# Spatial-weight sums by column blocks, attention without a forced end, and a z2 product among the last bands

## The chip, the cores and the metric

One core of one Trainium2 chip. The metric is device time of one execution, in microseconds (us); several executions of each kernel are timed in turn with the kernel before. Engines: PE is the tensor engine, DVE the vector engine, ACT the scalar engine, SP the engine whose queue issues nearly all loads and stores.

## The reference

Two blocks share 2048 tokens of width 1024, and a sigmoid gate mixes them:

```
g = sigmoid((x * gate_w).sum(-1))
A: qkv = x @ wqkv; 32 heads; each token attends to 8 earlier tokens, 2 apart; softmax; o @ wo
B: z = gelu(x @ w_in); z1 = z[..., :1792]; z2 = layernorm(z[..., 1792:])
   b = (z1 * (w_sp @ z2 + b_sp)) @ w_out
out = g * a + (1 - g) * b
```

w_sp is 2048 x 2048, the "spatial weights". Inputs and outputs are bfloat16.

## The kernel before

The large products run as Strassen-like quads: seven half-size products whose operands are sums and differences, made on DVE. Each product of a quad ends in a PSUM bank that ACT or DVE must read before PE may use that bank again (in the trace of the kernel before, PE waits 0.3 us each for L421, L474 and L487). In the profiles L403 is a matmul of such a product; L421, L427 and L487 are ACT's and L474 is DVE's work on its bank. A band set is a batch of attention's score products (L355), which ACT copies (L363), and which are stored to HBM (band_d) and loaded again. L1178 (L1192 in the changed kernel) is the gelu of z1. The stages overlap: attention of head group g (eight groups, four heads each) is computed on DVE and ACT while PE already projects the next group, then z2, then z1. Instruction order is fixed when the program is built: a list scheduler with a clock for each engine places DVE work between PE products.

z1 has seven steps, numbered here from the first to the seventh (fp = 0 to 6 in the code). Beside these, the spatial weights are loaded by eight transposing transfers and combined on DVE.

```python
def products():                      # attention: weights times v, then the tree of sums
    ...
    for ws in SPLIT[g > FINE]:       # FINE is -1: slices of 2, 2048 elements
        ... tt(p5[:, ws], in0[:, ws], in1[:, ws], ALU.mult)                # the "L677" of the profile
    for n, ws in enumerate([slice(0, 4)] if g <= FINE else [slice(0, 2), slice(2, 4)]):
        ... tt(a, a, b, ALU.add)                                           # L681
    ...                                                                    # L682, L686

BAND_AT = (1, 3, 6)                  # after which products of a quad a band set stands
...
return [tiles[0], band[1], tiles[1], band[0], tiles[2], band[2], tiles[3]] # group 7

def load_raw(c, a):                  # one of eight transposing loads of w_sp
    row = 4 * c + (a % 4) + 8 * (a // 4)
    inst = sync.dma_start_transpose(raw_slots[c][:, :, a, :], wsp_v[row])
...
z1s_slots = [... for o in (T1_OFF, R_OFF + 16384)]     # z1_quad uses z1s_slots[fp == 3]
...
RAW_AT = {2: {2: 0, 4: 1}, 3: {2: 2, 4: 3, 6: 4}, 4: {2: 5, 4: 6, 6: 7}}
for fp in range(NFH):
    ...
    if fp == SUMS:                   # the sixth step
        fill.extend((clock["PE"] + RAW_IN, 1.15, f) for f in wsp_sums(0, 0))
    ...
    run(z1_quad(fp, 0), z1_quad(fp, 1), hooks=hooks, step=lambda: z1_step(fp, at))
    if fp == DRAIN:                  # after the second step: all that is left of attention
        drain()
    ...                              # loads of w1, stores of z1
    if fp == NFH - 3:
        load_rows()                  # b_sp and og, after the fifth step
```

The gelus of all z1 steps but the fourth write one buffer, from which the step's result is stored to HBM (z_d); the next step's gelus must wait until that store has landed (5.6 us in two waits in the kernel before). And the weights land in the buffers that attention used, so no transpose may start before attention's last result (o_d) is stored (SP waits 4.8 us for it in the kernel before).

## Time and profile before

| | before |
|---|---|
| time, median of 3 runs (of 6, with the changed kernel) | 650.38 us (650.45) |
| span of the profiled run | 649.2 us |
| PE busy | 638.1 us, 98% |
| DVE / ACT busy | 519.3 / 297.8 us |
| listed PE waits between 50 and 640 us | 0.6 + 0.3 + 0.3 + 0.3 + 0.3 us |

PE is the bound nearly everywhere, so a change is judged by where PE stands on the clock, and by the waits that bind it.

The table "position" below is made so: the start of the same ACT copy out of PSUM (they follow PE's products) in one trace, less its start in the trace of the kernel before.

### The profile page before, as it was taken

To read this page: it belongs to the slowest core of one execution; us is meant where nothing else is said; L and a number is where in the kernel's file an instruction comes from. 1 tells how busy PE (TensorE), PEld (TensorE's weight loads), DVE (VectorE), ACT (ScalarE), POOL (GpSimd) and SP (SyncE) were. 2 spreads that over 40 slices of the span, in tenths; PEclk is the share of its full clock that TensorE was granted. 3 is DMA by queue.
4 is the path that set the end of the run, shared out by engine and by line. 5 is a ranking of instruction groups with operands and counts; after the bars stand their busy time and mean duration, and the time that the engine had idled before them with its cause. 6 is when DMAs were issued, how large, how long until landed. Compare 5 with 4: busy or idle time off the path is not lost.

```text
span 649.2 us, 11298 instructions
## 1 busy us (share of the span) xinstructions
PE 638.1 (98%) x4346; PEld 336.4 (52%) x4391; DVE 519.3 (80%) x816; ACT 297.8 (46%) x644; POOL 15.4 (2%) x27
## 2 busy tenths in 40 slices
PE   8999999999999999999999999999999999999997
PEld 4544467444445555444444444444444444868684
DVE  0357988999899999999988766987569999596952
ACT  3547677676776877799643121121121121212110
POOL 2210000000000000001000000000000000000000
PEclk9999999999999999999999999999999999999999
DMA  9979564798688012258994578469587383665401
GB/s 207 198 179 269 126 152 103 175 230 200 122 214 204 1 42 85 66 148 230 258 269 133 130 163 172 120 195 280 100 189 172 86 157 99 111 138 128 124 27 49
DMA packets 227174, 98.19 MB, mean 151 GB/s; under 512 B 174496, under 2 KB 214064, under 8 KB 227120
## 3 DMA queue, kind: packets, MB, share of 16 engines
q1 hardware_dynamic: 226256, 95.70, 61.2%
q0 software_dynamic: 576, 1.57, 0.9%
q8 instruction: 34, 0.56, 0.3%
q10 hardware_dynamic: 288, 0.20, 0.1%
q14 instruction: 20, 0.16, 0.1%
HBM read 44.31 MB, written 36.61 MB: 125 GB/s over the span
## 4 chain that ended last, share of the span: by engine, by line
PE 84%; ACT 4%; DVE 4%; DMA 4%; SPq 2%; issue 2%; ACTq 0%; DVEq 0%
PE psum_all L403 69%; PE psum_all L1487 8%; PE psum_all L293 4%; PE psum_all L303 2%; DMA band_d<-arena 2%; ACT arena L839 2%; PE psum_all L355 1%; DVE arena L677 1%; ACT arena L1178 1%; SPq L189 1%; DVE arena L681 1%; SPq L178 1%; DMA arena<-in_A_wqkv_dram 1%; SPq L194 1%; DVE psum_all L474 1%
## 5 line engine op out<-in xcount | busy, mean ns | idle before, releaser
L403 PE MATMUL psum_all<-arena 128*128 128x512 f16 (+6 forms) x2482 | 503.0, 362 | 3.4 <-issue 0.6
L403 PEld LDWEIGHTS <-arena 128*128 128x128 f16 (+1 forms) x2518 | 245.1, 98 | 253.8 <-issue 4.0
L677 DVE TENSOR_TENSOR arena<-arena,att_A 128x2048 f16<-128x2048 bf16 x64 | 75.5, 1219 | 0.3
L474 DVE TENSOR_TENSOR psum_all<-psum_all,arena 128x512 f32<-128x512 f32 (+1 forms) x78 | 51.0, 669 | 10.1 <-PE psum_all L403 8.3
L1487 PE MATMUL psum_all<-arena 128*128 128x256 f16 (+1 forms) x468 | 51.6, 273 | 0.0
L1487 PEld LDWEIGHTS <-arena 128*128 128x128 f16 x468 | 45.8, 98 | 5.5
L293 PE MATMUL psum_all<-arena 128*128 128x512 bf16 x183 | 42.0, 379 | 1.4 <-issue 0.8
L421 ACT COPY psum_all<-psum_all 128x512 f32<-128x512 f32 (+1 forms) x24 | 12.5, 521 | 66.8 <-PE psum_all L403 66.2
L784 ACT ACTIVATE arena<-psum_all 128x448 bf16<-128x448 f32 x64 | 34.3, 546 | 19.0 <-PE psum_all L403 9.0
L1178 ACT ACTIVATE arena<-psum_all 128x512 bf16<-128x512 f32 x56 | 31.4, 612 | 19.8 <-PE psum_all L403 9.0
L681 DVE TENSOR_TENSOR arena<-arena 128x2048 f16<-128x2048 f16 x32 | 37.9, 1218 | 0.0
L363 ACT CAST arena<-psum_all 128x1988 f16<-128x1988 f32 (+3 forms) x25 | 34.0, 1360 | 3.6 <-PE psum_all L355 3.4
L839 ACT ACTIVATE arena<-arena 128x896 bf16<-128x896 bf16 x32 | 30.9, 980 | 0.0
L546 DVE TENSOR_TENSOR arena<-arena 128x512 f16<-128x512 bf16 (+5 forms) x60 | 30.1, 534 | 0.3
L445 ACT COPY psum_all<-psum_all 128x512 f32<-128x512 f32 (+1 forms) x24 | 12.4, 519 | 37.2 <-PE psum_all L403 36.6
L293 PEld LDWEIGHTS <-arena 128*128 128x128 bf16 x192 | 18.1, 98 | 21.6 <-DMA arena<-in_A_wqkv_dram 0.7
L870 ACT CAST arena<-psum_all 128x512 bf16<-128x512 f32 x40 | 22.1, 592 | 12.5 <-DVE psum_all L474 9.6
L389 DVE TENSOR_TENSOR arena<-arena 128x2048 f16<-128x2048 bf16 x8 | 9.4, 1222 | 21.8 <-ACT gl_s L306 20.9
L427 ACT COPY arena<-psum_all 128x512 f32<-128x512 f32 (+1 forms) x24 | 12.7, 534 | 26.3 <-PE psum_all L403 22.5
L487 ACT COPY psum_all<-psum_all 128x512 f32<-128x512 f32 (+1 forms) x39 | 21.7, 570 | 6.6 <-PE psum_all L403 6.0
L432 ACT COPY psum_all<-psum_all 128x512 f32<-128x512 f32 (+1 forms) x24 | 12.5, 519 | 25.6 <-PE psum_all L403 23.0
L550 DVE TENSOR_TENSOR arena<-arena 128x1024 f16<-128x1024 f16 (+1 forms) x16 | 11.3, 714 | 15.7 <-PE psum_all L403 15.7
(113 smaller groups left out, 530.6 us busy)
## 6 DMA issues: line engine op xcount, KB each, us to landing
arena<-v_d SPq DMA_DIRECT2D x8, 960.0 KB, 7.1
z_d<-arena SPq DMA_DIRECT2D x14, 512.0 KB, 3.4
arena<-z_d SPq DMA_DIRECT2D x14, 512.0 KB, 4.1
zg_d<-arena SPq DMA_DIRECT2D x56, 128.0 KB, 2.2
arena<-zg_d SPq DMA_DIRECT2D x32, 224.0 KB, 3.2
band_d<-arena SPq DMA_DIRECT2D x28, 248.5 KB, 4.6
arena<-in_A_wqkv_dram SPq DMA_DIRECT2D x16, 256.0 KB, 4.3
o_d<-arena SPq DMA_DIRECT2D x4, 1024.0 KB, 6.3
```

Source lines behind the costliest of these rows:

```text
L293: nc.tensor.matmul(ps[:], w[:, t, kt, :], xT[:, kt, 512 * c:512 * (c + 1)], start=(kt == 0), stop=(kt == KT - 1))
L363: nc.scalar.copy(dst, src)
L403: nc.tensor.matmul(bank[:, 0:N], lhsT, rhs, start=(start and m == 0), stop=(m == n - 1), skip_group_check=True)
L474: last_add[0] = nc.vector.tensor_tensor(out[:, n], a[:, n], vs, ALU.add)
L546: return [lambda a=a: nc.vector.tensor_tensor(*a) for a in args]
L677: lambda ws=ws, in0=in0, in1=in1: tt(p5[:, ws], in0[:, ws], in1[:, ws], ALU.mult)), False
L681: lambda a=p3[:, ws], b=p3[:, ws.start + 4:ws.stop + 4]: tt(a, a, b, ALU.add)), not n
L784: nc.scalar.activation(z2[:, i + 8 * a, ZC * c:ZC * (c + 1)], bank[:, 0:ZC], ACT.Gelu_apprx_tanh, accum_out=s1[:, 4 * n + c:4 * n + c + 1])
L839: return nc.scalar.activation(junk, src, ACT.Square, accum_out=(s2, s2h)[x][:, n:n + 1])
L870: nc.scalar.copy((qT_slots, kT_slots)[t][g % 2][:, :, 256 * (c + 2 * x):256 * (c + 2 * x + 1)], bank[:].rearrange("p (n e) -> p e n", e=2))
L1178: last_gelu[0] = nc.scalar.activation(z1s[:, f, a, :], bank[:], ACT.Gelu_apprx_tanh)
L1487: nc.tensor.matmul(bank[:, h], l, r, start=(start and m == 0), stop=(m == len(ab) - 1), skip_group_check=True)
```

## The change

Its intent: to take out the small PE waits in groups 2 and 7, to let attention's DVE work run out among the z1 steps in place of a forced end that stops everything else, and to begin the sums of the spatial weights by column block, each as soon as its two loads have landed.

```diff
-                for ws in SPLIT[g > FINE]:
+                for ws in SPLIT[not wide[0]]:                 # wide in groups 5, 6, 7: 4096 elements
...
-            if n + 1 in BAND_AT:
+            if n + 1 in (BAND_AT if g != 2 else (1, 3, 5)):
...
-        return [tiles[0], band[1], tiles[1], band[0], tiles[2], band[2], tiles[3]]
+        early.append(z2_quad(*quads[0], 0))
+        return [tiles[0], band[1], tiles[1], lambda: next(early[0]), band[0], tiles[2], band[2], tiles[3]]
...
+        two = [z2_quad(*q, m) for m, q in enumerate(quads[n:n + 2])]
+        if n == 0:
+            two = [two[1], early[0]]
...
         if c == 0:
-            for n in (0, 4):        # halves
...
+            lo, hi = slice(P * part, P * part + P), slice(512 + P * part, 512 + P * part + P)
+            a, b, e, t1 = raw[:, 0:8, lo], raw[:, 0:8, hi], raw[:, 8:16, hi], t_sum[0][:, :, lo]
+            yield lambda: tt(t1, b, a, ALU.subtract)
+            yield lambda: tt(half[:, 0:8, hi], e, b, ALU.subtract)
...
     def z1_step(fp, at):
         step()
         at[0] += 1
+        since[0] += 1
+        if raws and since[0] >= 3 and not due and all(s[1] == () for s in streams):
+            load_raw(0, raws.pop(0))
+            since[0] = 0
+            if len(raws) % 2 == 0:
+                pair = 3 - len(raws) // 2
+                raw_in[0] = max(raw_in[0] + 4.5, clock["PE"] + 8.0, z3[0] + 8.0)
+                fill.extend((raw_in[0], 0.61, f) for f in wsp_sums(0, pair))
+                fill.sort(key=lambda x: x[0])
...
-    RAW_AT = {2: {2: 0, 4: 1}, 3: {2: 2, 4: 3, 6: 4}, 4: {2: 5, 4: 6, 6: 7}}
...
-        if fp == DRAIN:
-            drain()
```

`streams` are attention's three queues of DVE work: the first transpose is placed once they are empty, the next ones at least three products apart.

More of the change, by code (lines that the diff above doesn't have):

```diff
@@ L678, in products @@
                 multiplied.add((g, e))
-                for n, ws in enumerate([slice(0, 4)] if g <= FINE else [slice(0, 2), slice(2, 4)]):
+                for n, ws in enumerate([slice(0, 4)] if wide[0] else [slice(0, 2), slice(2, 4)]):
                     yield now, 0.068 + 0.533 * (ws.stop - ws.start), (
@@ L692, in products @@
             next_v()
+    wide = [False]
     SPLIT, FINE = [[slice(n * x, n * x + n) for x in range(8 // n)] for n in (4, 2)], FINE_TO
@@ L785, in z2_gelu, with z2_tile @@
                              accum_out=s1[:, 4 * n + c:4 * n + c + 1])
-    def z2_tile(i, a, m):
-        ps = low_bank()
+    def z2_tile(i, a, m, bank=low_bank):
+        ps = bank()
         pe(2 * T_Z)
@@ L912, in play_group @@
         return True
+    early = []
     def group_tiles(g):
@@ L917, in group_tiles @@
         else:
-            tiles = [lambda a=a, m=m: z2_tile(7, a, m) for m in range(2) for a in range(2)]
+            roles = bank_roles[0]
+            tiles = [lambda n=n: z2_tile(7, n % 2, n // 2, lambda: roles[3 - n % 2]) for n in range(4)]
         if g == 0:
@@ L1030 @@
         hold[0] = g == NG - 1
+        wide[0] = g in (5, 6, 7)
         paired = play_group(g)
@@ L1050 @@
             play(main[8 - (not g):])
+    wide[0] = False
     load_later(1, clock["PE"] + 3.0, 2.0)
@@ L1065, in quad_step @@
         def quad_step():
-            hold[0] = count[0] != 1
-            if n == 0 and count[0] == 0:
-                mark(bank_roles[1][1:3], ZC)
+            hold[0] = count[0] != 4
             step()
@@ L1073, in quad_step @@
                 square(*squares.pop(0), None)
-        run(*[z2_quad(*q) for q in quads[n:n + 2]], step=quad_step)
+        two = [z2_quad(*q, m) for m, q in enumerate(quads[n:n + 2])]
+        if n == 0:
+            two = [two[1], early[0]]
+            next(early[0])
+            quad_step()
+            mark(bank_roles[1][1:3], ZC)
+        run(*two, step=quad_step)
     hold[0] = False
@@ L1130, in wsp_sums @@
         if c == 0:
-            for n in (0, 4):
-                i, hi = slice(n, n + 4), slice(8 + n, 12 + n)
-                a, b, d, e = raw[:, i, 0:512], raw[:, i, 512:1024], raw[:, hi, 0:512], raw[:, hi, 512:1024]
-                t1, t2, t3 = (t[:, i] for t in t_sum)
-                if part == 0:
-                    yield lambda t1=t1, a=a, b=b: tt(t1, b, a, ALU.subtract)
-                    yield lambda b=b, e=e, h=half[:, i, 512:1024]: tt(h, e, b, ALU.subtract)
-                else:
+            if part == 4:
+                for n in (0, 4):
+                    i, hi = slice(n, n + 4), slice(8 + n, 12 + n)
+                    d, e = raw[:, hi, 0:512], raw[:, hi, 512:1024]
+                    t1, t2, t3 = (t[:, i] for t in t_sum)
                     yield lambda t1=t1, t2=t2, e=e: tt(t2, e, t1, ALU.subtract)
                     yield lambda t2=t2, t3=t3, d=d: tt(t3, d, t2, ALU.subtract)
+                return
+            lo, hi = slice(P * part, P * part + P), slice(512 + P * part, 512 + P * part + P)
+            a, b, e, t1 = raw[:, 0:8, lo], raw[:, 0:8, hi], raw[:, 8:16, hi], t_sum[0][:, :, lo]
+            yield lambda: tt(t1, b, a, ALU.subtract)
+            yield lambda: tt(half[:, 0:8, hi], e, b, ALU.subtract)
         elif part == 0:
@@ L1193 @@
     ready = [0]
+    raws, since, raw_in = [0, 4, 1, 5, 2, 6, 3, 7], [0], [0.0]
+    z3 = [0.0]
     def z1_step(fp, at):
@@ L1197, in z1_step @@
         at[0] += 1
+        since[0] += 1
[6 more added lines that the diff above has]
+                fill.extend((raw_in[0], 0.61, f) for f in wsp_sums(0, pair))
+                fill.sort(key=lambda x: x[0])
         if at[0] % 2 == 0 and squares:
@@ L1205, in z1_step @@
         if fp == NFH - 1 and at[0] == 2:
-            fill.extend((0.0, 1.15, f) for f in wsp_sums(0, 1))
+            fill.extend((0.0, 1.15, f) for f in wsp_sums(0, 4))
     mark([b[1] for b in bank_roles], 512, ZC)
@@ L1210 @@
     RAW_IN = 3.0
-    DRAIN, SUMS = 1, NFH - 2
-    RAW_AT = {2: {2: 0, 4: 1}, 3: {2: 2, 4: 3, 6: 4}, 4: {2: 5, 4: 6, 6: 7}}
+    SUMS = NFH - 2
     for fp in range(NFH):
@@ L1218 @@
         if fp == SUMS:
-            fill.extend((clock["PE"] + RAW_IN, 1.15, f) for f in wsp_sums(0, 0))
+            assert not raws
+        z3[0] = clock['PE'] + 12.0 * (3 - fp) + 12.0
         late = () if fp else [b[2] for b in bank_roles]
         at = [0]
-        hooks = {3: lambda: mark(late, 512, ZC), **{n: lambda a=a: load_raw(0, a) for n, a in RAW_AT.get(fp, {}).items()}}
+        hooks = {3: lambda: mark(late, 512, ZC)}
         if fp == 2:
```

## The prediction

Two inputs: the trace of the kernel before gives them as follows. The 0.07 us that a merge saves, an estimate: back to back, DVE instructions of 1024 elements start 0.60 us apart (two L550 take 1.29 us, one 0.69), those of 2048 elements 1.13 us (two L681 take 2.35 us, one 1.22), and 2 x 0.60 - 1.13 = 0.07. And PE's matmuls of 448 columns start 0.189 us apart (28 take 5.46 us, one 0.352), four 0.76 us. Of the stores behind transposes, those at 318.65 and 319.28 us landed 3.2 and 4.8 us after issue, but one at 306.44 us only after 7.2.

> **What bounds the kernel now.** I read the page first: engine totals, then the chain that ended last. Then the tensor engine's (PE's) own waits, the busy time in 10 us windows, and the timelines around each place the change touches.
>
> ```profile
> PE 638.1 (98%) x4346; PEld 336.4 (52%) x4391; DVE 519.3 (80%) x816; ACT 297.8 (46%) x644; POOL 15.4 (2%) x27
> ...
> PE 84%; ACT 4%; DVE 4%; DMA 4%; SPq 2%; issue 2%; ACTq 0%; DVEq 0%
> ```
>
> PE is busy 638.1 of 649.2 us, so all idle time is 11.1 us. The windows view puts 1.9 us of it in the first 10 us and 3.5 in the last; the change reaches neither. Between them PE streams nearly without a break: in the long products a 512-column matmul follows the other every 0.216 us. The order of instructions says that PE runs the same 4390 matmuls before and after. So the change can win only what PE waits for in the middle, and lose only by new waits. The PE waits that are in its reach:
>
> ```profile
> PE psum_all L355 <- ACT arena L363: 0.6, 1, 0.6
> ...
> PE psum_all L403 <- ACT psum_all L487: 0.3, 1, 0.3
> ...
> PE psum_all L403 <- DVE psum_all L474: 0.3, 1, 0.3
> ...
> PE psum_all L403 <- ACT psum_all L421: 0.3, 1, 0.3
> ```
>
> About 1.5 us in all, 0.23%: the most the change could win here, unless it also takes the small waits below the list.
>
> [...] at 331.8 us (below) an ACT instruction that waits for a store holds up all behind it. So I read each queue as a fixed order and ask which wait ends last. [...] stores issued behind weight transposes land behind them, 3 to 5 us after issue. [...] four 2048-element products take 4.62 us, a pitch of 1.13 us[...]. I use 0.07.
>
> **Part 1, group 2: third band set one product earlier.** PE waits there at 84.8 and 87.8 us, 0.35 and 0.25 us. The chain by time has, ahead of the second:
>
> ```profile
> 82.07 5.06 DMA band_d<-arena
> ...
> 87.55 0.44 ACT psum_all L421
> ...
> 88.03 27.33 PE psum_all L403 x200
> ```
>
> The first v quad's scratch overlaps the buffer of the *second* band set, whose store lands at 87.13. The change moves the third. The first wait vanishes, but PE then arrives sooner at the second and waits longer; it still resumes at 88.0. Worth 0.0.
>
> **Part 2, group 7: first z2 product among the bands, and wide DVE instructions.**
>
> ```profile
> 178.77 0.27 PE L355 MATMUL psum_all<-arena 32*64 32x64 bf16 x16 [0.62 <-ACT arena L363]
> ...
> 184.01 4.62 DVE L677 TENSOR_TENSOR arena<-arena,att_A 128x2048 f16<-128x2048 bf16 x4
> ...
> 188.88 1.16 DVE L474 TENSOR_TENSOR psum_all<-psum_all,arena 128x448 f32<-128x448 f32 x2
> ...
> 189.56 6.71 PE L403 MATMUL psum_all<-arena 128*128 128x448 f16 x33 [0.27 <-DVE psum_all L474]
> ```
>
> Four matmuls of 448 columns[...] move into the 0.62 us gap, so PE is 0.6 ahead at 178.9. It then meets the DVE, which is full here. Nine merges (six of L677, three of L681) save 0.07 each; four lie after the last starved stretch of DVE (169.4), 0.3 us. L474 also comes ahead of L661 (0.3). So the L474 that PE needs ends at 188.9 instead of 189.5, but PE, one product of its order short of where it waited before, arrives at 187.8 and waits 1.1. Adding up the order from there, with two more L474 in time: the product that started at 193.64 starts at about 193.4. Net -0.2.
>
> **Part 3, turn from z2 to z1 (259.7 us).** PE waits 0.28 us for ACT, behind gelus whose source, an L474, stood behind L682 and L686. In the new order it stands ahead of them (0.1 sooner), and the next one stands ahead of an L681 (some 0.15 us of PE wait near 263). Net -0.2.
>
> **Part 4, attention without a forced end, and the weight sums.** The sums are the same element count: eight column-block instructions of 1024 elements in place of four of 2048, at 0.60 instead of 1.13 us: 0.3 us more DVE, where DVE has room. What matters is when the raw weights may be loaded. They overwrite attention's buffers, so the first transpose waits for the last attention store. Before, the forced end puts attention's last L686 ahead of the third z1 step's sums:
>
> ```profile
> 293.64 0.54 SPq L189 DMA_DIRECT2D o_d<-arena  x1
> ...
> 299.08 4.58 SPq L194 DMA_TRANSPOSE arena<-in_B_w_sp_dram  x2
> ...
> 307.06 11.49 SPq L194 DMA_TRANSPOSE arena<-in_B_w_sp_dram  x3
> ...
> 319.90 8.23 SPq L194 DMA_TRANSPOSE arena<-in_B_w_sp_dram  x3
> ...
> 328.23 1.20 SPq L189 DMA_DIRECT2D z_d<-arena  x2
> ...
> 331.83 0.60 ACT L1178 ACTIVATE arena<-psum_all 128x512 bf16<-128x512 f32 x1 [4.38 <-DMA z_d<-arena]
> ...
> 333.68 3.30 ACT L1178 ACTIVATE arena<-psum_all 128x512 bf16<-128x512 f32 x6 [1.25 <-DMA z_d<-arena]
> ...
> 338.10 0.57 ACT L487 COPY psum_all<-psum_all 128x512 f32<-128x512 f32 x1 [0.26 <-PE psum_all L403]
> ```
>
> In the new DVE order the last L682 and L686 stand behind the L474 that reads the third step's fifth product (of seven) in its second quad. That product ends at 297.0 (297.4 before, less 0.4 gained): +0.15 latency, L474 0.6, L682 1.25, L686 0.7: attention ends at 299.6, so the store starts 6 us later than at 293.6, and the first transpose at 305.0 (the 5.4 us between store and transpose kept). Before, eight transposes, two w1 loads and four z stores took 299.08 to 328.18, with DMA above 90% busy in nearly every slice. After, one w1 load goes ahead of them, which spares 2.3 us (its spacing in landings): 29.1 - 2.3 = 26.8. So the stores of the fifth z1 step issue at 331.8, not 328.2, and land near 335.4 and 337.3, not 331.8 and 333.6.
>
> The gelus of the sixth step write the buffer that these stores read. ACT already waits 4.38 and 1.25 us for them; PE does not, as ACT catches up before the seventh step. The slack: from the second landing, seven gelus at 0.54, then L487 (0.57) and latency: 4.5 us, against a PE that starts the seventh step's third product at 337.1 + 4 x 0.863 = 340.5. So the landing may be 340.5 - 4.5 - 333.6 = 2.4 us later. It will be 3.7 later on the clock and 0.4 more against a PE that gained: 4.1 - 2.4 = 1.7, say +1.6 us of new PE wait near 340 us. The sums themselves do not stall PE: the first needs the fourth step's store, landing near 326.8, and PE needs what is queued behind it by 331.4, with 3.9 us of work between.
>
> Sum: 0.0 - 0.2 - 0.2 + 1.6 = +1.2 us.
>
> **Rivals.** (a) *All hidden, a small win.* The late transposes still end in time: if the transposes run faster than I took, or the slack is larger, +1.6 becomes 0 and the result is 650.38 - 0.4 = 650.0; with all the listed waits gone, 649. For it: every PE gap here was small and hidden before. Against it: ACT waited 5.6 us on these stores already. (b) *The queue becomes the bound twice.* The fourth step's stores come behind five transposes, and the first sum waits for them in the strict DVE order; its slack is 0.7 us. If transposes take 10% longer, DVE holds up the sixth step by 1 us and PE waits in both: 653. (c) *DVE frees PE.* If the wide instructions let DVE run ahead, all its waits vanish. Against it: they save 0.6 us of 519, and order fixes where L474 stands. Part 4 is the stake; I give its late landing 7 in 10.
>
> **Range and chances.** 650.38 - 0.4 + 0.7 x 1.6 = 651.1 us. Low: 649.4, rival (a) with most waits gone. High: 652.8, rival (b). Two per cent is 13 us; nothing here is of that size: faster 0.01, same 0.98, slower 0.01.
>
> **What would show it right or wrong.** PE: no wait before L355 near 178, one near 1 us for DVE L474 near 188; still about 0.2 to 0.9 us waiting for ACT L421 near 88. SP queue: o_d store near 299.6 instead of 293.6, first transpose near 305, the last stores behind transposes near 332. ACT: waits for z_d stores that sum to near 9 us instead of 5.6. PE: a new wait of 1 to 2 us near 340 us for ACT L487. If PE has no wait between 300 and 350 us, part 4's slack or rate is wrong; if the o_d store is not later by 5 us, its reading of the order is wrong. If the time is under 649.4, I missed idle time inside PE's busy time.

## The result, and the profile after

The changed kernel took 651.89 us (median of 6 runs, 650.71 to 652.54), beside 650.45 us for the kernel before in the same rounds. The ratio is 1.0015 with a 95% interval of 1.0002 to 1.0029. Ratios here are the mean time of one kernel's runs over that of the other's of the same rounds, so not quite the ratio of the medians quoted. By the 2% rule it is "the same"; the small loss is nevertheless just clear of the noise.

The engine totals and the shares of the chain in the changed kernel's page, beside those in the prediction:

```profile
PE 641.7 (99%) x4391; PEld 336.4 (52%) x4391; DVE 519.7 (80%) x811; ACT 297.8 (46%) x644; POOL 15.4 (2%) x27
...
PE 83%; DVE 6%; ACT 4%; SPq 2%; issue 2%; DMA 2%; DVEq 0%; ACTq 0%
```

PE's 3.6 us more of busy time are no loss: this trace has all 4391 matmuls. The list of PE's waits says more (total, times, longest):

```profile
PE psum_all L403 <- ACT arena L1192: 1.7, 3, 1.0
...
PE psum_all L403 <- DVE psum_all L474: 0.7, 2, 0.4
```

The waits for L355 at 178 us, for L421 at 88 us and for L487 at 260 us are gone. In their place PE waits 1.7 us for L1192, the gelu of z1. The timeline around it, with attention's last store, the first transpose, and the fifth step's stores on the SP queue ahead of it:

```profile
299.02 0.54 SPq L189 DMA_DIRECT2D o_d<-arena  x1
...
304.33 2.34 SPq L194 DMA_TRANSPOSE arena<-in_B_w_sp_dram  x1
...
322.28 8.76 SPq L194 DMA_TRANSPOSE arena<-in_B_w_sp_dram  x3
...
331.14 1.21 SPq L189 DMA_DIRECT2D z_d<-arena  x2
...
336.47 0.60 ACT L1192 ACTIVATE arena<-psum_all 128x512 bf16<-128x512 f32 x1 [10.12 <-DMA z_d<-arena]
...
337.12 1.02 PE L403 MATMUL psum_all<-arena 128*128 128x512 bf16 x4 [1.00 <-ACT arena L1192]
...
337.72 3.54 ACT L1192 ACTIVATE arena<-psum_all 128x512 bf16<-128x512 f32 x7 [0.65 <-DMA z_d<-arena]
...
338.37 1.02 PE L403 MATMUL psum_all<-arena 128*128 128x512 bf16 x4 [0.23 <-ACT arena L1192]
...
339.83 8.38 PE L403 MATMUL psum_all<-arena 128*128 128x512 f16 x37 [0.45 <-ACT arena L1192]
```

Read it backwards. PE restarts at 337.12 because a gelu that ended at 337.07 freed its bank. That gelu waited 10.12 us for the fifth step's store. The store left SP only at 331.14, although the last gelu of its data ended at 324.6: it stood behind three transposes that kept SP for 8.76 us. Three transposes stood ahead of it in the kernel before too (the prediction shows the lines: 8.23 us from 319.90, the store at 328.23), and PE did not wait there. New is that they start 2.4 us later and that the store leaves 2.9 us later. The first transpose could not start before 304.33 (299.08 before), since it waited for the store of attention at 299.02 (293.64 before).

Where PE stands against the kernel before, in us (negative is ahead), at five points of the kernel before's clock, and the span:

| trace | 108 | 265 | 303 | 327 | 351 | span |
|---|---|---|---|---|---|---|
| changed | -0.29 | -1.08 | -1.10 | -1.09 | +1.36 | +0.95 |
| e8, changed again | -0.50 | -0.70 | -0.72 | -0.72 | +2.44 | +2.02 |
| e1, parts 1 to 3 | -0.51 | -0.78 | +0.28 | +0.28 | +0.28 | -0.12 |
| e2, part 4 alone | -0.08 | -0.78 | -0.67 | -0.70 | +3.62 | +3.63 |
| e3 | -0.51 | -1.63 | -1.65 | -1.65 | +3.43 | +3.01 |
| e4 | -0.26 | -1.04 | +0.02 | +5.83 | +6.03 | +5.75 |
| e5 | -0.42 | +0.35 | +0.33 | +0.34 | +0.37 | -0.05 |
| e6 | -0.44 | -1.44 | -1.44 | -1.44 | -1.44 | -1.85 |
| e7, part 1 alone | -0.32 | -0.14 | -0.14 | -0.14 | -0.14 | -0.06 |
| e9, e6 again | -0.09 | -0.12 | -0.14 | -0.14 | -0.14 | -0.55 |

So the change gains 1.1 us up to the z1 stage and loses 2.45 between 327 and 351 us. From 351 us to the last products nothing more moves.

### The profile page after: what moved, and what is told of

Read it like the earlier page. It is cut to its first block, busy times and chain, and to the rows that moved or that the text cites. A ratio compares the mean times of both kernels' runs of the same rounds, so it can differ in the third digit from the quotient of the medians.

```text
span 650.1 us, 11336 instructions
## 1 busy us (share of the span) xinstructions
PE 641.7 (99%) x4391; PEld 336.4 (52%) x4391; DVE 519.7 (80%) x811; ACT 297.8 (46%) x644; POOL 15.4 (2%) x27
## 4 chain that ended last, share of the span: by engine, by line
PE 83%; DVE 6%; ACT 4%; SPq 2%; issue 2%; DMA 2%; DVEq 0%; ACTq 0%
PE psum_all L403 68%; PE psum_all L1511 8%; PE psum_all L293 4%; PE psum_all L303 2%; DVE arena L677 2%; ACT arena L1192 2%; ACT arena L840 1%; SPq L194 1%; PE psum_all L355 1%; DVE arena L681 1%; DMA z_d<-arena 1%; DVE psum_all L474 1%; SPq L178 1%; DVE arena L546 1%; DMA arena<-in_A_wqkv_dram 1%
## 5 line engine op out<-in xcount | busy, mean ns | idle before, releaser
L677 DVE TENSOR_TENSOR arena<-arena,att_A 128x2048 f16<-128x2048 bf16 (+1 forms) x58 | 75.1, 1329 | 0.2
L474 DVE TENSOR_TENSOR psum_all<-psum_all,arena 128x512 f32<-128x512 f32 (+1 forms) x78 | 51.3, 670 | 11.3 <-PE psum_all L403 9.4
L421 ACT COPY psum_all<-psum_all 128x512 f32<-128x512 f32 (+1 forms) x24 | 12.5, 521 | 66.5 <-PE psum_all L403 65.7
L1192 ACT ACTIVATE arena<-psum_all 128x512 bf16<-128x512 f32 x56 | 31.2, 614 | 23.1 <-DMA z_d<-arena 10.8
L681 DVE TENSOR_TENSOR arena<-arena 128x2048 f16<-128x2048 f16 (+1 forms) x29 | 37.6, 1329 | 0.0
L487 ACT COPY psum_all<-psum_all 128x512 f32<-128x512 f32 (+1 forms) x39 | 21.8, 574 | 6.4 <-PE psum_all L403 5.7
L427 ACT COPY arena<-psum_all 128x512 f32<-128x512 f32 (+1 forms) x24 | 12.7, 533 | 26.3 <-PE psum_all L403 22.5
L303 PE MATMUL psum_all<-arena 128*128 128x385 bf16 x128 | 22.3, 327 | 0.8 <-DMA arena<-in_A_x_dram 0.5
```

The lines of the kernel that those rows point to most:

```text
L303: nc.tensor.matmul(ps[:, 0:VP + 1], xT[:, kt, i * P:(i + 1) * P], wvp[:, kt, :], start=(kt == 0), stop=(kt == KT - 1))
L474: last_add[0] = nc.vector.tensor_tensor(out[:, n], a[:, n], vs, ALU.add)
L677: lambda ws=ws, in0=in0, in1=in1: tt(p5[:, ws], in0[:, ws], in1[:, ws], ALU.mult)), False
L681: lambda a=p3[:, ws], b=p3[:, ws.start + 4:ws.stop + 4]: tt(a, a, b, ALU.add)), not n
L1192: last_gelu[0] = nc.scalar.activation(z1s[:, f, a, :], bank[:], ACT.Gelu_apprx_tanh)
```

## The experiments

Each kernel was timed in five rounds. Theory A, from the trace: the one SP queue carries transposes and z1 stores in order; attention's late end delays the transposes and with them the fifth step's stores, which stand behind the last three, and the gelus, then PE, wait for these.

### e1: all but part 4

Edit: the kernel before with the upper half of the change (parts 1 to 3: `wide`, the band sets of group 2, the early quad). Left as they were:

```python
    RAW_AT = {2: {2: 0, 4: 1}, 3: {2: 2, 4: 3, 6: 4}, 4: {2: 5, 4: 6, 6: 7}}   # in place of the rule in z1_step
...
            fill.extend((clock["PE"] + RAW_IN, 1.15, f) for f in wsp_sums(0, 0))  # sums by halves, at the sixth step
...
        if fp == DRAIN:
            drain()
```

> Parts 1 to 3 of the change alone (third band set earlier in group 2, early z2 quad, wide DVE instructions, the turn); attention's forced end, fixed hooks for the transposes and the sums by halves are as in the kernel before. Theory A (part 4 alone costs, parts 1 to 3 keep what the changed kernel's trace shows them to win, 1.2 us by 290 us): 649.2 us, 0.9982 of before, no wait of PE for a gelu near 340 us, and the stores of the fifth z1 step land near 331 to 333 us. Rival B (the loads and stores of the z1 stage end at a time of their own, so what PE gains early is lost there whatever the forced end): PE waits 0.5 to 1.2 us near 335 to 340 us and the time is 650.3 us.

Measured: 650.57 us beside 650.83; ratio 0.9990 (0.9977 to 1.0003). No wait near 340 us, so the loss there is part 4's: rival B falls. But theory A was only half right, since the gain did not survive either. By 291 us PE was 0.79 ahead, and at the forced end it lost 1.07:

```profile
293.27 0.69 DVE L686 TENSOR_TENSOR arena<-arena 128x1024 f16<-128x1024 f16 x1
...
295.08 1.29 DVE L474 TENSOR_TENSOR psum_all<-psum_all,arena 128x512 f32<-128x512 f32 x2
...
295.82 2.54 PE L403 MATMUL psum_all<-arena 128*128 128x512 f16 x11 [0.92 <-DVE psum_all L474]
```

In the new order four L677 stand between the preceding L474 and the forced end, where the kernel before had three (4.62 against 3.48 us), so the forced end now makes L474 late. This is what dropping the forced end is for: the changed kernel passes 295 us with no loss. It then pays on the SP queue.

### e2: part 4 alone

Edit: the kernel before with the lower half of the change only:

```diff
+        if raws and since[0] >= 3 and not due and all(s[1] == () for s in streams):
+            load_raw(0, raws.pop(0))
...                                   # and the sums by column block
-    RAW_AT = {2: {2: 0, 4: 1}, 3: {2: 2, 4: 3, 6: 4}, 4: {2: 5, 4: 6, 6: 7}}
-        if fp == DRAIN:
-            drain()
```

> Part 4 alone on the kernel before: no forced end of attention, transposes by the new rule, sums by column blocks. Theory A: attention's last store leaves some 6 us later than before (near 300 us), the stores of the fifth z1 step are issued near 331 to 332 us, PE waits 1 to 2.5 us near 337 to 341 us, 652.3 us (1.003 of before). Rival B: PE has no gain to lose here, so it waits less than 0.5 us and the time is 650.5 us.

Measured: 654.72 us beside 650.83; ratio 1.0062 (1.0049 to 1.0076). The stage loses 4.3 us, and the wait is another than in the changed kernel: DVE waits for the store of the *fourth* step.

```profile
328.02 0.69 DVE L1142 TENSOR_TENSOR arena<-arena 128x1024 f16<-128x1024 bf16 x1 [4.13 <-DMA z_d<-arena]
...
333.84 11.46 PE L403 MATMUL psum_all<-arena 128*128 128x512 f16 x45 [2.58 <-DVE psum_all L474]
```

L1142 is the first column sum; it writes where the fourth step's stores read. The second of these two stores was issued behind a further transpose (at 324.10; at 319.28 in the kernel before), landed at 327.80. DVE ran nothing else in the 4.13 us of its wait; L474, which stands behind L1142 in its order, started at 333.10, and PE at 333.84. This is the prediction's rival (b). The step lost 1.7 us more than the 2.6 of the wait, for a reason that the windows view shows; each line gives the stretch and its length, then the busy time of PE, PEld, DVE, ACT and POOL with their counts, then the granted clock, the DMA share and GB/s:

```profile
333.80:337.00 3.20, 3.16 (x8) 1.13 (x8) 3.15 (x5) 1.04 (x3) 0.00 (x0) 0.50 0.96 270
...
337.00:345.00 8.00, 8.00 (x38) 3.61 (x37) 6.95 (x10) 4.57 (x8) 0.00 (x0) 1.00 0.49 181
```

After the wait, the granted clock was 0.50 and the next matmuls came every 0.427 us (the starts of their weight loads), for some 3 us; before the wait it was 0.216 us (25 matmuls in 5.56 us, one 0.379).

### e3: the last two transposes behind the stores

```diff
-        if raws and since[0] >= 3 and not due and ...
+        if raws and (fp >= 5 or len(raws) > 2) and since[0] >= 3 and not due and ...
-        if fp == SUMS:
-            assert not raws
```

> The changed kernel with one edit: the last two of the eight transposes are held back until the sixth z1 step, so the stores of the fifth step are issued ahead of them. Theory A (these stores are late because they stand behind transposes in the SyncE queue): they are issued near 326.5 us instead of 331.1, land near 330 to 331 us, ACT waits at most 5 us for them instead of 10.8, the PE waits of 1.7 us near 337 to 340 us go, 649.6 us. Rival C (the DMA engines are simply full of bytes until some 335 us, and order does not matter): the stores still land after 335 us, PE still waits over 1 us, 651.5 us or more.

Measured: 654.48 us beside 650.83; ratio 1.0056 (1.0040 to 1.0071): a miss in time, and yet the mechanism came out as theory A said. The fifth step's stores left at 326.40 and the first landed at 329.61, so bytes were not the limit (rival C falls), and the gelus waited 5.1 us and no longer held PE. The wait moved:

```profile
341.69 0.69 DVE L1153 TENSOR_TENSOR arena<-arena 128x1024 f16<-128x1024 bf16 x1 [4.71 <-DMA arena<-in_B_w_sp_dram]
...
346.10 3.61 PE L403 MATMUL psum_all<-arena 128*128 128x512 f16 x16 [3.15 <-DVE psum_all L474]
```

The last two transposes were issued only from 329.92 on, behind the loads of rows, and the second landed at 341.59; the last pair of column sums waits for them at the head of DVE's queue. PE waited for an L474 twice more, 0.38 us at 330.70 (behind a pair of column sums) and 1.06 us at 350.77. From start to start the three are 0.55, 3.32 and 1.22 us, the 5.08 us that the stage lost.

### e4: the forced end again

```diff
         run(z1_quad(fp, 0), z1_quad(fp, 1), hooks=hooks, step=lambda: z1_step(fp, at))
+        if fp == 1:
+            drain()
```

> The changed kernel with one line added: attention's forced end after the second z1 step, as before; transposes still go by the new rule. Theory A (the late end of attention is what pushes the transposes): attention's last store near 292 to 294 us, first transpose near 298, all eight transposes issued before the stores of the fifth step are ready, no PE wait near 340 us, 649.3 us. Rival D (the new rule for the transposes, three steps apart, is what puts the stores behind them): PE still waits 1 to 2 us near 337 to 341 us, 651 us or more.

Measured: 656.26 us beside 650.83; ratio 1.0082 (1.0070 to 1.0095), the worst of all. Attention ended early (o_d store at 293.73, first transpose at 299.35) as theory A said. But the new rule then places five transposes ahead of the second of two loads of w1, the z1 weights (issued at 314.60), and DVE's sums of that load wait:

```profile
319.13 1.55 DVE L546 TENSOR_TENSOR arena<-arena 128x512 f16<-128x512 bf16 x4 [6.24 <-DMA arena<-in_B_w_in_dram]
...
323.86 2.76 PE L403 MATMUL psum_all<-arena 128*128 128x512 f16 x7 [3.96 <-DVE psum_all L474]
```

After this wait the granted clock was low again (0.55 between 323.9 and 327.5 us, with 10 matmuls where e3 had 18), so the step lost 5.8 us. After e3's wait of 3.15 us it was 1.00 (346.1 to 350.0 us); what lowers it is not shown.

Neither A nor D as I had put them: it is the order of *all* transfers on the one queue that decides which instruction waits, and every order that I had tried only moved the wait. e1 also shows 1.07 us lost at 295 us by the forced end, and e4 the same (-1.04 to +0.02).

Part 4 has three pieces: no forced end, the new rule for the transposes, and sums by column block. No run has one of them alone. That the delay comes from attention's late end is therefore read from the trace (its store 5.4 us and the first transpose 5.25 us later), not isolated by an edit.

### e5: stores, transposes, rows

From e3's wait follows the next order: rows behind the last transposes.

```diff
-        if fp == NFH - 3:
-            load_rows()
+        if fp == SUMS:
+            hooks[6] = load_rows
```

> As e3 (last two transposes behind the stores of the fifth z1 step), with the two loads of rows (bias and og), which stood ahead of the last two transposes there, moved behind them. e3 showed that the stores then leave at 326.4 us and the gelus no longer hold PE, but the last pair of column sums waited 4.7 us for transposes landing at 341.6 us and PE 3.2 us for the L474 behind them. Theory A (order in the one SyncE queue decides which wait there is): the last two transposes land near 334 us, DVE waits for none of them, PE loses at most 0.4 us after 300 us and keeps about 1.1 us of what it gained before: 649.5 us. Rival E (the transposes cost the time wherever they stand, as the DMA engines are full): the eighth still lands after 338 us and PE waits over 1 us for DVE: 652 us or more.

Measured: 650.71 us beside 651.34; ratio 0.9992 (0.9974 to 1.0009). In its trace PE loses nothing between 303 and 351 us (+0.33 to +0.37), and DVE waits for no transpose: theory A holds for the stage, rival E falls. Not all came as expected: the seventh transpose landed at 336.87 us, not near 334, and ACT waited 4.43 us for a store at 344.33, without holding PE. In the traced run (650.9 us) the expected gain is missing for a reason far from this edit; the other five runs have no trace. PE waited 1.96 us near 187 us, where the program is the same in the changed kernel, e3, e5 and e6:

```profile
169.82 0.29 DVE L640 TENSOR_TENSOR att_m<-att_L 128x256 f16<-128x256 f16 x1 [2.74 <-DMA att_L<-band_d]
...
189.38 0.92 PE L403 MATMUL psum_all<-arena 128*128 128x448 f16 x4 [1.96 <-DVE psum_all L474]
```

L640 is the first DVE instruction that needs a band load; from it DVE works without a break to the L474 that PE needs. The start of L640 and PE's idle time between 186 and 194 us in all traces with part 2, in the order of L640 (us):

| | e3 | e6 | changed | e4 | e1 | e8 | e9 | e5 |
|---|---|---|---|---|---|---|---|---|
| L640 starts | 167.84 | 168.05 | 168.39 | 168.44 | 168.69 | 168.77 | 169.36 | 169.82 |
| PE idle | 0.06 | 0.20 | 0.39 | 0.39 | 0.90 | 0.98 | 1.16 | 1.96 |

The idle time follows the start of L640, and so the landing of the load, which differs by 2 us from run to run of the same instructions. In the old order it is so too: 168.61, 169.26, 169.40 us with 0.00, 0.58, 0.41 us idle (e2, e7, before), though there the 0.62 us at 178 us come on top.

### e6: the same, with the column sums later

e3 and e5 had one pair of sums between the evictions of a z1 step and its L474. Planned 4.5 us later, the second to fourth pair stand behind the sixth step's L474.

```diff
-        z3[0] = clock['PE'] + 12.0 * (3 - fp) + 12.0
+        z3[0] = clock['PE'] + 12.0 * (3 - fp) + 16.5
```

> As e5, and the column sums are planned 4.5 us later, so that the second to fourth pair stand behind the L474 of the sixth z1 step's third product instead of ahead of it. Theory A: the PE wait of 0.4 us near 330 us that e3 showed goes too, 649.2 us, below both kernels. If the later sums instead run into the first product of the spatial stage, PE waits 0.5 to 2 us near 348 to 352 us and the time is 650 to 651 us.

Measured: 649.93 us beside 651.34; ratio 0.9977 (0.9963 to 0.9991): below the kernel before. As in e5, PE waits nowhere in the stage, and it keeps its 1.44 us to the end:

```profile
325.75 1.21 SPq L189 DMA_DIRECT2D z_d<-arena  x2
...
329.70 0.60 ACT L1192 ACTIVATE arena<-psum_all 128x512 bf16<-128x512 f32 x1 [3.69 <-PE psum_all L403]
...
331.08 0.60 ACT L1192 ACTIVATE arena<-psum_all 128x512 bf16<-128x512 f32 x1 [0.79 <-DMA z_d<-arena]
```

The first gelu of the sixth step waits for PE, no longer for a store. So it did in e5 (at 331.47). What the later sums add is therefore not shown: the two traces are 1.79 us apart at 265 us already, where the programs are the same, and 1.81 us at 351.

### e7: part 1 alone

```diff
-            if n + 1 in BAND_AT:
+            if n + 1 in (BAND_AT if g != 2 else (1, 3, 5)):
```

> Part 1 alone on the kernel before (the third band set one product earlier in group 2). From the four traces with this part, PE is 0.4 us ahead by 108 us. Theory F (DVE is a second limit up to the forced end of attention, at a time of its own near 293.7 to 294 us): PE waits 0.3 to 0.5 us near 295 us for L474, and is level with the kernel before after it, 650.7 us beside 650.8. Rival G (what PE gains early is kept): no wait near 295 us, 650.4 us.

Measured: 650.82 us beside 651.34; ratio 0.9989 (0.9977 to 1.0001). Part 1 does gain 0.41 us in group 2 (+0.09 to -0.32). There was no wait near 295 us: theory F, a wall of DVE at a fixed time, falls. DVE moved with PE here; the wall in e1 and e4 comes from the order of instructions there, as told under e1. Of the 0.41 us, 0.18 were lost again at the waits for L474 near 189 us, where landings decide.

### e8 and e9: the changed kernel and e6 side by side

No edit. Both ran on one chip with the same runs of the kernel before.

> The changed kernel once more, unedited, beside e9 on the same chip. If its loss is the z1 stage's (2.45 us in its first trace) against some 1.1 us won before it: 1.0015 of before again, within 0.0015, and again 1.3 to 2 us of PE waits for gelus near 337 to 340 us, while the wait near 187 us is anything from 0 to 2 us, by the landing of group 7's band load.

> The version of e6 once more, unedited, beside e8. Theory A: 0.9977 of before again, within 0.0015, so 2 to 3 us under e8, with no PE wait over 0.2 us between 300 and 350 us. If e6 was a lucky run: 0.999 or more.

Measured: the changed kernel 653.73 us, e6's version 650.41 us, the kernel before 651.84 us; ratios 1.0021 (0.9992 to 1.0051) and 0.9980 (0.9944 to 1.0016). This chip scattered more (of its six runs over 654 us, five have a mean granted clock of 0.997, while all its runs below have 0.999 or 1.000), so that neither ratio alone is clear of 1, but both came out where they had been. e8's trace shows the 1.7 us of waits for gelus once more, and beside it 0.57 us for L474 behind a column sum that waited 1.94 us for the fourth step's stores, as the timeline of e8 has it:

```profile
327.93 0.69 DVE L1153 TENSOR_TENSOR arena<-arena 128x1024 f16<-128x1024 bf16 x1 [1.94 <-DMA z_d<-arena]
...
331.81 5.34 PE L403 MATMUL psum_all<-arena 128*128 128x512 f16 x24 [0.57 <-DVE psum_all L474]
```

So the changed kernel has two waits on that queue, and the second binds in some runs only. e9 shows no PE wait over 0.1 us between 300 and 350 us; its 1.16 us near 187 us took the gain of its profiled run.

## Why the prediction was right or wrong

Predicted +1.2 us, weighted 651.1 in a range of 649.4 to 652.8; measured 651.89 with 650.45 before. Direction, size and cause were right. That the sum came so near is in part luck: in the first trace the terms are -0.29 (part 1), -0.79 (parts 2 and 3), +2.45 (part 4) and -0.41 us (the end), where the prediction had 0.0, -0.4, +1.6 and nothing. Two of its readings were loose, without effect on the sum: its 11.1 us of idle time include what 45 missing matmul records leave, and PE runs 4391 matmuls, not 4390.

**Part 1, "worth 0.0": wrong by 0.4 us.** The failed step is "it still resumes at 88.0". It took the landing of the second band set's store, 87.13 us, as fixed. In the nine traces with part 1 the ACT copy L427 that waits for this store started between 86.04 and 86.94 us, in the two without (before, e2) at 87.23 and 87.15, and PE's wait for L421 behind it is gone. e7 isolates it: 0.41 us. Why the store lands sooner was not tested.

**Part 2, "waits 1.1", "net -0.2": a number where there is a distribution.** The wait came where I said and for L474, but as 0.06 to 1.96 us in eight traces (0.39 in the first). I had copied one trace's landing of the band load; with nearly the same one (L640 at 169.36 us, 169.40 before) e9 shows 1.16 us. From 108 to 265 us, parts 2 and 3 together made -0.43 us on the mean of the eight traces with them (from -1.12 to +0.77), beside -0.17 in the three without (before as 0.00, e2 -0.70, e7 +0.18). The predicted -0.4 fits, but the scatter is larger than the term, so its size stays open.

**Part 3, "net -0.2": wrong sign, small.** From 249 to 265 us PE lost 0.10 us in the changed kernel, and as much in e1. It now waits 0.36 us for L474, which stands behind three L677 (3.50 us in a row), in place of 0.28 us for ACT. I had looked at what L474 overtakes, not at what is still ahead of it.

**Part 4: the chain was right, link by link.** Expected and measured: attention's store 299.6 and 299.02; first transpose 305.0 and 304.33; fifth step's stores issued 331.8 and 331.14; ACT's waits for them "near 9 us" and 10.8; PE's new wait 1.6 and 1.7. Two steps of it were off. First, "the slack: from the second landing ... then L487": PE did not wait for L487 near 340 us but for the first gelu at 336.1, since a gelu's bank is needed again before the gelus have caught up. I had followed the wrong one of two landings to PE. Second, the cost: the stage lost 2.45 us, not 1.6. The wait list measures from the modelled end of the last matmul (a 512-column matmul is listed with 0.379 us, where the next starts after 0.216), and is short by about 0.17 us each time. From start to start, the four longest excesses over the normal pitch are 1.17, 0.39, 0.61 and 0.24 us, 2.4 together, where the list says 1.00, 0.23 and 0.45.

**"The sums themselves do not stall PE", slack 0.7:** right in the first trace (DVE waited 1.28 us, PE not at all), wrong in e8 (1.94 us, PE 0.57). Rival (b) was thus no rival but the neighbour: the same queue, one step's stores earlier.

**"The change reaches neither" of the two ends: wrong by 0.4 us.** In every trace with parts 2 and 3 the span ends 0.28 to 0.42 us sooner than PE's position at 351 us would have it (the last two columns of the table); in e2 and e7, without them, 0.01 and 0.08 us later. The traces tell where: up to SP's last wait, 2.46 to 2.48 us after the start of the last matmul, all agree; the closing instructions of the program end 1.3 us after that in before, e2 and e7, and 0.9 to 1.0 us after it in the others. No run tells why.

What the prediction did not ask is whether the loss has to be. The traces of e5, e6 and e9 show that it does not: with the stores ahead of the last two transposes and the rows behind them, attention may run out without a forced end and the z1 stage loses nothing.

## What to carry to other kernels

When a forced end is dropped, list everything that waits for what it ended, then everything that stands behind *that* in the same DMA queue: here a 5 us later end of attention cost nothing on DVE (PE stood at -1.10 us at 303 us and at -1.09 at 327), but the transposes waited for it, and a store behind them, which a gelu needed, left 2.9 us later. Moving one transfer in a busy queue can move the wait to the next reader (e3: DVE waited 4.71 us for a transpose; e4: 6.24 us for a load of w1); plan the order of all transfers from the times at which their readers reach the head of their own engine's queue. And before a term of a few tenths of a microsecond is believed, look at the same wait in several traces: a landing that moves by 2 us between runs outweighs it.
